# A retention layer in front of a Mish MLP: the first tile's q and k loads split over token groups, and the first tile made of four batches

## The chip, the cores and the metric

The kernel runs on one core of a Trainium2 chip. The metric is the device time in microseconds (us) of one execution; lower is better. The core has TensorE (PE, whose weight loads are listed apart as PEld), VectorE (DVE), ScalarE (ACT), GpSimd (POOL) and SyncE (SP). SP, ACT and POOL can issue DMAs; "SPq", "ACTq" and "POOLq" in the profile are those issuing queues.

## The reference

For each of 8 batches and 8 heads there are 576 tokens with 64 numbers each in q, k and v (float32). The attention has no softmax: it is a retention with a decay per head.

```python
scores = q @ k^T / sqrt(64)                       # 8 batches, 8 heads, 576 x 576
gamma  = 1 - 2 ** (-5 - h)                        # one per head h
ret    = scores * where(i >= j, gamma ** (i - j), 0)
x      = (ret @ v), heads joined to 512 numbers   # 4608 tokens x 512
h      = x @ w_in                                 # 512 -> 2048
out    = (h * tanh(softplus(h))) @ w_out          # 2048 -> 512, float32
```

## The kernel before

**Chunks and tiles.** The 576 tokens of a batch are cut into four chunks of 128 and a rest of 64. A list `chunks` orders all 36 chunks (two rests make one chunk). Two neighbouring chunks are a pair `m`: the same tokens of two batches. Four chunks are a tile `t` of 512 tokens, on which the MLP works; there are nine tiles. In the list before, the chunks 0 to 7 are the tokens 0, 128, 256 and 384 of the batches 0 and 1. So the first tile (chunks 0 to 3) holds tokens 0 to 255 of two batches.

**What is done to a chunk.** The decay is split into a factor for q and one for v, so a chunk needs only a triangular mask. The steps have one letter each:

- P (`step_p`): DVE multiplies q by its factor and casts it to bf16, into `qks`.
- V (`step_v`): v times its factor into `vs`. For the first tile it is POOL that does it, and it first casts k into `qks`.
- T (`step_t`): q and k are transposed, on PE into PSUM and then copied by ACT into `qkT`.
- S (`step_s`): 8 score matmuls into a PSUM tile `sc`, then DVE multiplies by the mask into `sm`.
- O (`step_o`): 8 matmuls `vs` x `sm`, for a chunk that isn't the first of its batch 8 more with the state of the earlier chunks (`ssb`), then a copy into the tile's `xT`.
- N (`step_n`): only for the pairs 0 and 1: k is transposed back into `ks` (8 PE transposes and a copy of 128x1024).
- K (`step_k`): a pair's k and v are added to its batches' state (16 PE matmuls into the PSUM tile `st`, two ACT copies into `ssb`). N must come before it for the pairs 0 and 1.

**The MLP.** `g1` is 4 matmuls against `w_in` and a Mish on ACT into `gT`; `g1_some` and `g1_chunk` do the same for 3 chunks or one. `g2` is `gT` against `w_out`, then a DVE copy and a store.

**Order.** The kernel runs under a manual schedule: each engine does its instructions in the order in which the program writes them, and each queue issues its DMAs in that order. First come the loads of the first tile, then constants, then a loop over the four first chunks (the head), and then everything else (the body): a pass of `g1` over the first tile into which N and K of pair 1 and the chunk 4 are woven, `g1_chunk` passes for the chunks 4 to 7, and alternating `g1` and `g2` with the later chunks.

**Loads.** The first tile is loaded by SP (`load_first`, L128 to L137), all 20 DMAs ahead of everything else. Its q and k are laid out so that one partition holds four consecutive tokens of one head (1 KB): partitions 0 to 31 are head 0 (or 1), 32 to 63 head 2 (or 3), and so on. This is one DMA for the even and one for the odd heads:

```python
in_=heads[b, e, :, ds(i0, P), :].rearrange("p (g t) d -> p g (t d)", t=4)
```

The outer loop of the source is over four heads `p`, the next over 32 token groups `g`. v is loaded with one token in a partition. All other loads are issued by POOL, in the order w_in (0,2), w_in (2,2), then w_in (4,4), w_in (8,4), chunk 4's q, k and v, w_in (12,2), w_in (14,2), chunks 5 to 7, w_out, and the pairs 4, 5, ... The POOL engine also does V of the first tile, so these loads stand behind it in POOL's order: w_in (0,2) behind V of chunk 2, w_in (2,2) and all later ones behind V of chunk 3.

**Filling PE.** `keep_warm(n)` issues n matmuls of 128x512 on zeros: 9 ahead of the head, then 2 before and 3 after each S.

Of the kernel before, what the change touches and what calls it, by code (L numbers as in the profile page):

```python
# [17 lines left out]
def kernel(  # L18
# [31 lines left out]

    chunks = []
    for g in range(0, B, 4):
        for b in (g, g + 2):
            for c in range(4):
                chunks += [((b + u, P * c, P),) for u in range(2)]
        chunks += [((g + u, 512, 64), (g + 2 + u, 512, 64)) for u in range(2)]
    n_chunks = len(chunks)
    n_pairs = n_chunks // 2
# [2 lines left out]
    def place(n):  # L61
        return chunks[n][0][1] // P
# [65 lines left out]
    def load_first(n):  # L128

        b, i0, _ = chunks[n][0]  # L130
        m, u = divmod(n, 2)
        for x, src in (("q", q), ("k", k)):
            heads = src.rearrange("b (p e) s d -> b e p s d", e=2)
            for e in range(2):
                nc.sync.dma_start(out=pairs[m][x][:, u, ds(4 * e, 4), :].rearrange("p t d -> p (t d)"),  # L135
                                  in_=heads[b, e, :, ds(i0, P), :].rearrange("p (g t) d -> p g (t d)", t=4))
        nc.sync.dma_start(out=pairs[m]["v"][:, u], in_=v[b, :, ds(i0, P), :].rearrange("h p d -> p h d"))  # L137

    for n in range(NCH):
        load_first(n)  # L140

# [4 lines left out]
    def keep_warm(n):  # L148
        for _ in range(n):
            nc.tensor.matmul(warm, lhsT=idle[:, 0:P], rhs=idle, start=True, stop=True)  # L150

    keep_warm(9)


    pos1 = consts.tile([P, 2, 4], F32)
    nc.gpsimd.iota(pos1, pattern=[[P, 2], [1, 4]], base=0, channel_multiplier=4,
                   allow_small_or_imprecise_dtypes=True)
    ident = consts.tile([P, P], BF16)
    make_identity(nc, ident)

    pos = consts.tile([P, 5], F32)
    nc.gpsimd.iota(pos, pattern=[[P, 5]], base=0, channel_multiplier=1,
                   allow_small_or_imprecise_dtypes=True)
    nc.gpsimd.iota(pos[64:P, 4:5], pattern=[[1, 1]], base=512, channel_multiplier=1,
                   allow_small_or_imprecise_dtypes=True)
    ex = consts.tile([P, 5, H], F32)
    for h in range(H):
        nc.vector.tensor_scalar(ex[:, :, h], pos, math.log(1.0 - 2.0 ** (-5.0 - h)), None, op0=OP.mult)

    lg1 = consts.tile([P, 2], F32)  # L170
    off1 = consts.tile([P, 1], F32)
    for a in range(NP):
        rows = ds(32 * a, 32)
        nc.vector.memset(off1[rows], 128.0 * a)
        for e in range(2):
            nc.vector.memset(lg1[rows, e:e + 1], math.log(1.0 - 2.0 ** (-5.0 - 2 * a - e)))
    ex1 = consts.tile([P, 2, 2, 4], F32)
    for e in range(2):
        nc.vector.tensor_scalar(ex1[:, :, e, :], pos1, off1, lg1[:, e:e + 1], op0=OP.subtract, op1=OP.mult)
    gq1 = consts.tile([P, 2, 2, 4], F32)  # L180
    nc.scalar.activation(gq1, ex1, AX.Exp)
    gq = consts.tile([P, 5, H], F32)
    gv = consts.tile([P, 5, H], F32)
    nc.scalar.activation(gq, ex, AX.Exp)
    nc.scalar.activation(gv, ex, AX.Exp, scale=-1.0)
    first = consts.tile([P, 1], F32)
    nc.scalar.activation(first, pos[:, 0:1], AX.Mish)
    nc.vector.tensor_scalar(gq, gq, 1.0 / math.sqrt(D), None, op0=OP.mult)
    nc.vector.tensor_scalar(gq1, gq1, 1.0 / math.sqrt(D), None, op0=OP.mult)

    mask = consts.tile([P, P], F32)
    mask2 = consts.tile([P, P], F32)
# [25 lines left out]
    def step_p(m, u0=0, nu=2):  # L218

        r = pairs[m]  # L220
        u = ds(u0, nu)
        if m < NCH // 2:
            nc.vector.tensor_tensor(by_lines(r["qks"][:, 0, u0]), by_heads(r["q"][:, u0]),
                                    gq1[:, place(2 * m)].unsqueeze(3).to_broadcast([P, 2, 4, D]), op=OP.mult)
            return
        g = gq[:, place(2 * m), :].unsqueeze(1).unsqueeze(3).to_broadcast([P, nu, H, D])
        nc.vector.tensor_tensor(r["qks"][:, 0, u], r["q"][:, u], g, op=OP.mult)  # L227

    def step_v(m, u0=0, nu=2):

        r = pairs[m]
        u = ds(u0, nu)
        if "vs" not in r:
            r["vs"] = tok.tile([P, 2, H, D], BF16, name="vs")
        g = gv[:, place(2 * m), :].unsqueeze(1).unsqueeze(3).to_broadcast([P, nu, H, D])
        eng = nc.vector
        if m < NCH // 2:
            eng = nc.gpsimd
            eng.tensor_copy(by_lines(r["qks"][:, 1, u0]), by_heads(r["k"][:, u0]))  # L239
        eng.tensor_tensor(r["vs"][:, u], r["v"][:, u], g, op=OP.mult)  # L240

    def step_t(n):

        m, u = divmod(n, 2)
        r = pairs[m]
        if "qk" not in r:
            r["qk"] = tr.tile([P, 2, 2, NP, P], BF16, name="qkT", bufs=3)
        if n >= NPE:
            nc.scalar.dma_start_transpose(out=r["qk"].rearrange("p i u n t -> p (i u n) t"),  # L249
                                          in_=r["qks"].rearrange("p i u h d -> p (i u h d)"))  # L250
            return
        if n < NCH:
            tp = ps_h.tile([P, 2, NP, P], BF16, name="hp")
            for i in range(2):
                lines = r["qks"][:, i, u].rearrange("p h d -> p (h d)")
                for t in range(4):
                    nc.tensor.transpose(tp[:, i, :, ts(t, 32)], lines[:, ts(t, P)], ident)  # L257

                nc.scalar.copy(r["qk"][:, i, u].rearrange("p n (g t) -> p n g t", t=4),
                               tp[:, i].rearrange("p n (t g) -> p n g t", t=4))  # L260
            return
        tp = ps_sc.tile([P, 4, NP, P], BF16, name="sc")[:, 0:2]
        for i in range(2):
            flat = r["qks"][:, i, u].rearrange("p h d -> p (h d)")
            for p in range(NP):
                nc.tensor.transpose(tp[:, i, p, :], flat[:, ts(p, P)], ident)  # L266
        nc.scalar.copy(r["qk"][:, :, u], tp)  # L267

    def step_n(m):

        r = pairs[m]
        kp = ps_h.tile([P, 2, NP, P], BF16, name="hp")
        for u in range(2):
            for p in range(NP):
                nc.tensor.transpose(kp[:, u, p, :], r["qk"][:, 1, u, p, :], ident)
        r["ks"] = tok.tile([P, 2, H, D], BF16, name="ks", bufs=2)
        nc.scalar.copy(r["ks"].rearrange("p u h d -> p u (h d)"), kp.rearrange("p u n t -> p u (n t)"))

    def step_s(n):

# [35 lines left out]
    def step_o(n):  # L316

        t, s = divmod(n, NCH)
        m, u = divmod(n, 2)
        qk, vs = pairs[m]["qk"], pairs[m]["vs"]  # L320
        sc, sm = pairs[m][u]
        ot = sc[:, 0]
        start = True
        off = 0
        for b, i0, ni in chunks[n]:
            if i0 > 0:
                for p in range(NP):
                    for e in range(2):
                        nc.tensor.matmul(ot[ds(64 * e, 64), p, ds(off, ni)], lhsT=st_sb[b, i0][:, p, e, :],  # L329
                                         rhs=qk[:, 0, u, p, ds(off, ni)],  # L330
                                         start=(start and p == 0), stop=False, skip_group_check=True)
                start = False
            off += ni
        for p in range(NP):
            for e in range(2):
                nc.tensor.matmul(ot[ds(64 * e, 64), p, :], lhsT=vs[:, u, 2 * p + e, :], rhs=sm[:, e, p, :],  # L336
                                 start=(start and p == 0), stop=True, skip_group_check=True)
        if s == 0:
            xts[t] = xp.tile([P, KC, NCH * P], BF16, name="xT")
        nc.vector.tensor_copy(xts[t][:, :, ts(s, P)], ot)  # L340


    gts = {}
# [73 lines left out]
    def one(n, steps):  # L417
        m, u = divmod(n, 2)
        for step in steps:
            if step in "PV":  # L420
                {"P": step_p, "V": step_v}[step](m, u, 1)
            else:
                {"T": step_t, "S": step_s, "O": step_o}[step](n)

    one(0, "PVT")
    for n in range(NCH):
        last = n == NCH - 1
        keep_warm(2)
        if not last:
            one(n + 1, "P")  # L430
        one(n, "S")
        if n == 1:
            step_n(0)
        keep_warm(3)
        if not last:
            one(n + 1, "VT")
            if n > 0:
                load_w_in(2 * n - 2, 2)
            one(n, "O")
            if n == 1:  # L440
                step_k(0)
    load_w_in(4, 4)
    load_w_in(8, 4)
    load_single(4)
# [14 lines left out]
    g1_chunk(3, 0)  # L459
    for i in range(4, nF):  # L460
        if i == 6:
            step_n(1)
        elif i == 8:
            step_k(1)
        elif i == 12:
            one(4, "PVT")
        elif i == 14:
# [24 lines left out]
    def visit(m, w):  # L492

        n = 2 * m
        if w == 0:
            step_p(m)
            step_v(m)
            if 2 * m + 2 < NPE:
                load(m + 4)
        elif w == 2:  # L500
            one(n, "T")
        elif w == 3:
            one(n + 1, "T")
# [88 lines left out]
```

## Time and profile before

| | |
|---|---|
| median of 14 runs (lowest to highest) | 337.33 us (335.22 to 338.87) |
| the profiled execution, its own time | 336.15 us |
| its span | 334.4 us |
| PE busy | 308.7 us (92%) |
| DVE, ACT, POOL busy | 130.8, 126.1, 79.9 us |
| DMA | 43.38 MB moved, 130 GB/s over the span |
| first `g1` matmul on a full tile (L351) | starts at 42.80 us |

The profile is of one execution. Its span runs from the first to the last event on the core; the execution's own time is 1.75 us longer, and the median of the runs is 1.18 us above that. "Busy" counts an engine's instructions; the rows of the timeline and the stage table give times from the span's start. In the stage table "DMA share" is the mean busy share of 16 DMA engines (transfers that overlap in one engine can take it above 1), and the last column is what they moved.

### The profile page before, as it was taken

What the parts mean: (1) busy time and instruction counts of PE and PEld (TensorE: products, weight loads), DVE (VectorE), ACT (ScalarE), POOL (GpSimd) and SP (SyncE); (2) the same over time, 40 slices, a digit from 0 to 9 for tenths busy, and PEclk for the clock granted to TensorE, in tenths of its full rate; (3) what the DMA queues carried; (4) which work ended last, traced back from release to release, by engine and by line L of the source; (5) the groups of instructions that cost most, each with busy time, mean ns of one, the idle gap of its engine ahead of it and who ended that gap; (6) DMA issues with size and microseconds to landing.
All of it is one profiled execution on the core that took longest, in us unless ns stands there. A gap on an engine that the chain in (4) does not pass through costs nothing.

```text
span 334.4 us, 6026 instructions
## 1 busy us (share of the span) xinstructions
PE 308.7 (92%) x2599; PEld 160.5 (48%) x2637; DVE 130.8 (39%) x176; ACT 126.1 (38%) x206; POOL 79.9 (24%) x101
## 2 busy tenths in 40 slices
PE   5466689999999999999999999999999999999996
PEld 1142345896455555444454545444554544444444
DVE  3233214620667467535445262626272723000121
ACT  4132366662234564233442434243433432333300
POOL 2232867635442102140404304050000000000000
PEclk9977999999999999999999999999999999999999
DMA  2335899999999904969598797999241411000023
GB/s 82 109 115 104 123 230 201 207 224 198 246 205 242 210 32 96 194 83 203 143 199 128 173 171 148 139 165 154 61 90 37 110 39 42 33 31 33 31 63 94
DMA packets 75594, 43.38 MB, mean 130 GB/s; under 512 B 59568, under 2 KB 66992, under 8 KB 75568
## 3 DMA queue, kind: packets, MB, share of 16 engines
q0 software_dynamic: 43104, 25.17, 50.8%
q1 hardware_dynamic: 11520, 12.45, 12.2%
q10 hardware_dynamic: 20944, 5.38, 9.9%
q8 instruction: 20, 0.33, 0.4%
q14 instruction: 6, 0.05, 0.0%
HBM read 36.70 MB, written 9.44 MB: 138 GB/s over the span
## 4 chain that ended last, share of the span: by engine, by line
PE 78%; SPq 7%; DMA 5%; ACT 3%; ACTq 3%; DVE 2%; issue 1%; POOL 1%
PE hp L351 30%; PE ops L389 29%; SPq L135 6%; PE hp L389 5%; PE hp L374 4%; PE sc L287 3%; DMA vraw<-in_v_dram 3%; ACTq L249 3%; DMA w_in_t<-in_moe_w_in_dram 3%; PE sc L329 2%; PE sc L336 2%; PE sc L266 2%; PE st L308 1%; ACT gT L353 1%; PE hp L401 1%
## 5 line engine op out<-in xcount | busy, mean ns | idle before, releaser
L351 PE MATMUL hp<-xT,w_in_t 128*128 128x512 bf16 x468 | 123.0, 380 | 5.2 <-DMA w_in_t<-in_moe_w_in_dram 3.1
L353 ACT ACTIVATE gT<-hp 128x512 bf16<-128x512 f32 x124 | 73.9, 598 | 133.5 <-PE hp L351 107.5
L389 PE MATMUL ops<-w_out_t,gT 128*128 128x512 bf16 x476 | 121.3, 379 | 0.7
L389 PEld LDWEIGHTS <-gT 128*128 128x128 bf16 x560 | 54.2, 98 | 64.7 <-issue 0.8
L351 PEld LDWEIGHTS <-w_in_t 128*128 128x128 bf16 x496 | 46.0, 98 | 58.3 <-DMA w_in_t<-in_moe_w_in_dram 3.3
L409 DVE COPY res<-ops 128x512 f32<-128x512 f32 x30 | 20.7, 691 | 129.7 <-PE ops L389 129.7
L290 DVE TENSOR_TENSOR sm<-sc,mask 128x1024 bf16<-128x1024 f32 x36 | 42.6, 1216 | 19.2 <-PE sc L287 19.2
L515 POOL COPY seen<-qkT 1x1 bf16<-1x1 bf16 x10 | 1.8, 177 | 127.0 <-DMA qkT<-qks 127.0
L340 DVE CAST xT<-sc 128x512 bf16<-128x512 f32 x36 | 23.5, 686 | 16.6 <-PE sc L336 15.8
L312 ACT ACTIVATE ssb<-st,diag 128x512 bf16<-128x512 f32 x32 | 20.2, 684 | 10.2 <-PE st L308 10.0
L227 DVE TENSOR_TENSOR qks<-qraw,gq 128x1024 bf16<-128x1024 f32 (+1 forms) x18 | 19.7, 1096 | 9.2 <-DMA qraw<-in_q_dram 9.2
L104 POOL DMA_DIRECT2D qraw<-in_q_dram x16 | 17.2, 1076 | 19.8 <-DVE qks L227 12.8
L240 DVE TENSOR_TENSOR vs<-vraw,gv 128x1024 bf16<-128x1024 f32 (+1 forms) x18 | 19.8, 1099 | 0.9 <-DMA vraw<-in_v_dram 0.9
L104 POOL DMA_DIRECT2D vraw<-in_v_dram x16 | 17.3, 1088 | 6.0 <-DMA w_out_t<-in_moe_w_out_dram 2.5
L389 PE MATMUL hp<-w_out_t,gT 128*128 128x512 bf16 x76 | 18.0, 379 | 0.5 <-issue 0.5
L104 POOL DMA_DIRECT2D qks<-in_k_dram x16 | 17.2, 1082 | 5.1 <-PE hp L374 3.2
L267 ACT COPY qkT<-sc 128x1024 bf16<-128x1024 bf16 x12 | 12.2, 1013 | 14.6 <-PE sc L266 14.6
L374 PE MATMUL hp<-xT,w_in_t 128*128 128x128 bf16 x272 | 16.7, 219 | 0.0
L374 PEld LDWEIGHTS <-w_in_t 128*128 128x128 bf16 x272 | 15.4, 98 | 0.7 <-issue 0.2
L257 PE MATMUL hp<-ident,qks 128*128 128x128 bf16 x32 | 3.6, 242 | 12.1 <-POOL qks L239 9.3
L150 PE MATMUL ops<-idle 128*128 128x512 bf16 x27 | 12.8, 613 | 1.8 <-DVE idle L145 1.3
L336 PE MATMUL sc<-sm,vs 128*64 128x128 bf16 x288 | 14.1, 224 | 0.0
(63 smaller groups left out, 155.6 us busy)
## 6 DMA issues: line engine op xcount, KB each, us to landing
out_dram<-res SPq DMA_DIRECT2D x31, 256.0 KB
qraw<-in_q_dram POOLq DMA_DIRECT2D x12, 512.0 KB, 7.2
vraw<-in_v_dram POOLq DMA_DIRECT2D x12, 512.0 KB, 9.0
qks<-in_k_dram POOLq DMA_DIRECT2D x12, 256.0 KB, 7.7
qraw<-in_q_dram POOLq DMA_DIRECT2D x8, 256.0 KB, 9.8
vraw<-in_v_dram POOLq DMA_DIRECT2D x8, 256.0 KB, 8.3
w_out_t<-in_moe_w_out_dram POOLq DMA_DIRECT2D x4, 512.0 KB, 11.8
qraw<-in_q_dram SPq DMA_DIRECT2D x8, 128.0 KB
```

The lines of the kernel that those rows point to most:

```text
L104: nc.gpsimd.dma_start(out=t[ds(off, ni)].rearrange("p u h d -> p (u h) d"), in_=src[ds(b, 2), :, ds(i0, ni), :].rearrange("b h p d -> p (b ...
L135: nc.sync.dma_start(out=pairs[m][x][:, u, ds(4 * e, 4), :].rearrange("p t d -> p (t d)"), in_=heads[b, e, :, ds(i0, P), :].rearrange("p (g ...
L240: eng.tensor_tensor(r["vs"][:, u], r["v"][:, u], g, op=OP.mult)
L290: nc.vector.tensor_tensor(sm.rearrange("p e n i -> p (e n) i"), sc.rearrange("p e n i -> p (e n) i"), (mask if len(chunks[n]) == 1 else ma ...
L312: nc.scalar.activation(ssb[:, :, :, e, :], st, AX.Copy, scale=diag[:, e:e + 1])
L336: nc.tensor.matmul(ot[ds(64 * e, 64), p, :], lhsT=vs[:, u, 2 * p + e, :], rhs=sm[:, e, p, :], start=(start and p == 0), stop=True, skip_gr ...
L340: nc.vector.tensor_copy(xts[t][:, :, ts(s, P)], ot)
L351: nc.tensor.matmul(hp, lhsT=w_in_t[:, c, ts(f, P)], rhs=xts[t][:, c, :], start=(c == 0), stop=(c == KC - 1))
L353: nc.scalar.activation(gts[t][:, f, :], hp, AX.Mish)
L374: nc.tensor.matmul(hp[:, j, :], lhsT=w_in_t[:, c, ts(4 * fb + j, P)], rhs=xts[t][:, c, ts(s, P)], start=(c == 0), stop=(c == KC - 1))
L389: nc.tensor.matmul(ops, lhsT=gts[t][:, f, ts(s, P)], rhs=w_out_t[:, f, :], start=(f == 0), stop=(f == nF - 1))
L409: copy(ot, ops)
```

## The change

1. **Layout of the first tile's q and k.** The source's outer loop becomes the 32 token groups, the inner one the four heads. The partition of a row is then 4 x group + head pair, where it was 32 x head pair + group. The factors for q (`gq1`) are built for that layout: from the partition number's last two bits and eight compares and a sum on DVE, in place of memsets. The PSUM tile of T is written in whole 128-column blocks, and ACT's copy reads it in another order.
2. **Queue of the first tile's v.** ACT issues it, not SP. Chunk 0 is loaded at the start, chunk 1 behind ACT's exponentials, and chunks 2 and 3 in the head's loop, behind T of the chunks 0 and 1. SP's DMAs wait for nothing.
3. **Order of chunks.** The pair (batches 2 and 3, tokens 0 to 127) becomes pair 1; the pairs after it move back by one, up to the former pair 4. The first tile is then the first 128 tokens of four batches, and none of its chunks needs a state.
4. **N and K leave the head.** N of pair 0, K of pair 0 and N of pair 1 stand in the `g1` pass at i = 6, 8 and 9; K of pair 1 stands in `visit(5, 2)`, some 60 us later. N's copy moves from ACT to DVE and its PSUM tile from the pool of `hp` to that of `sc`. `vs` of the first tile has two buffers of its own.
5. **Small moves.** V is split into C (the cast of k) and V. w_in (2,2) is issued between C and V of chunk 3. The copy of O in the first tile goes from DVE to ACT. `keep_warm` goes to 12 ahead of the head and 4 and 3 around each S. The constants are built in another order.

```diff
-        for b in (g, g + 2):
-            for c in range(4):
-                chunks += [((b + u, P * c, P),) for u in range(2)]
+        order = [(b, c) for b in (g, g + 2) for c in range(4)]
+        if g == 0:
+            order.insert(1, order.pop(4))
+        for b, c in order:
+            chunks += [((b + u, P * c, P),) for u in range(2)]
...
-                                  in_=heads[b, e, :, ds(i0, P), :].rearrange("p (g t) d -> p g (t d)", t=4))
-        nc.sync.dma_start(out=pairs[m]["v"][:, u], in_=v[b, :, ds(i0, P), :].rearrange("h p d -> p h d"))
-    for n in range(NCH):
-        load_first(n)
+                                  in_=heads[b, e, :, ds(i0, P), :].rearrange("p (g t) d -> g p (t d)", t=4))
+        nc.scalar.dma_start(out=pairs[m]["v"][:, u], in_=v[b, :, ds(i0, P), :].rearrange("h p d -> p h d"))
+    load_first(0)
...
-    keep_warm(9)
+    keep_warm(12)
...
+    nc.vector.tensor_scalar(line, line, 3, None, op0=OP.bitwise_and)
+    nc.vector.tensor_copy(off1, line)
+    for a in range(NP):
+        for e in range(2):
+            nc.vector.tensor_scalar(own[:, e, a:a + 1], off1, float(a),
+                                    math.log(1.0 - 2.0 ** (-5.0 - 2 * a - e)), op0=OP.is_equal, op1=OP.mult)
+    nc.vector.tensor_reduce(out=lg1, in_=own, op=OP.add, axis=mybir.AxisListType.X)
...
+    load_first(1)
...
-                    nc.tensor.transpose(tp[:, i, :, ts(t, 32)], lines[:, ts(t, P)], ident)
+                    nc.tensor.transpose(tp[:, i, t, :], lines[:, ts(t, P)], ident)
-                               tp[:, i].rearrange("p n (t g) -> p n g t", t=4))
+                               tp[:, i].rearrange("p t (g n) -> p n g t", n=NP))
...
-        kp = ps_h.tile([P, 2, NP, P], BF16, name="hp")
+        kp = ps_sc.tile([P, 4, NP, P], BF16, name="sc")[:, 0:2]
-        nc.scalar.copy(r["ks"].rearrange("p u h d -> p u (h d)"), kp.rearrange("p u n t -> p u (n t)"))
+        nc.vector.tensor_copy(r["ks"].rearrange("p u h d -> p u (h d)"), kp.rearrange("p u n t -> p u (n t)"))
...
-        nc.vector.tensor_copy(xts[t][:, :, ts(s, P)], ot)
+        (nc.scalar.copy if t == 0 else nc.vector.tensor_copy)(xts[t][:, :, ts(s, P)], ot)
...
-    one(0, "PVT")
+    one(0, "PCVT")
     for n in range(NCH):
         last = n == NCH - 1
-        keep_warm(2)
+        if n + 2 < NCH:
+            load_first(n + 2)
+        keep_warm(4)
         if not last:
             one(n + 1, "P")
         one(n, "S")
-        if n == 1:
-            step_n(0)
         keep_warm(3)
         if not last:
-            one(n + 1, "VT")
-            if n > 0:
-                load_w_in(2 * n - 2, 2)
+            one(n + 1, "C")
+            if n == 2:
+                load_w_in(2, 2)
+            one(n + 1, "V")
+            if n == 1:
+                load_w_in(0, 2)
+            one(n + 1, "T")
             one(n, "O")
-            if n == 1:
-                step_k(0)
...
         if i == 6:
+            step_n(0)
+        elif i == 8:
+            step_k(0)
+        elif i == 9:
             step_n(1)
-        elif i == 8:
-            step_k(1)
...
         elif w == 2:
+            if m == 5:
+                step_k(1)
             one(n, "T")
```

More of the change, by code (lines that the diff above doesn't have):

```diff
@@ L150, in keep_warm @@
             nc.tensor.matmul(warm, lhsT=idle[:, 0:P], rhs=idle, start=True, stop=True)
-    keep_warm(9)
-    pos1 = consts.tile([P, 2, 4], F32)
-    nc.gpsimd.iota(pos1, pattern=[[P, 2], [1, 4]], base=0, channel_multiplier=4,
+    keep_warm(12)
+    line = consts.tile([P, 1], mybir.dt.int32)
+    nc.gpsimd.iota(line, pattern=[[0, 1]], base=0, channel_multiplier=1)
+    pos1 = consts.tile([P, 4], F32)
+    nc.gpsimd.iota(pos1, pattern=[[1, 4]], base=0, channel_multiplier=1,
                    allow_small_or_imprecise_dtypes=True)
-    ident = consts.tile([P, P], BF16)
-    make_identity(nc, ident)
     pos = consts.tile([P, 5], F32)
@@ L165 @@
                    allow_small_or_imprecise_dtypes=True)
+    ident = consts.tile([P, P], BF16)
+    make_identity(nc, ident)
+    nc.vector.tensor_scalar(line, line, 3, None, op0=OP.bitwise_and)
+    off1 = consts.tile([P, 1], F32)
+    nc.vector.tensor_copy(off1, line)
+    own = consts.tile([P, 2, NP], F32)
+    for a in range(NP):
+        for e in range(2):
+            nc.vector.tensor_scalar(own[:, e, a:a + 1], off1, float(a),
+                                    math.log(1.0 - 2.0 ** (-5.0 - 2 * a - e)), op0=OP.is_equal, op1=OP.mult)
+    lg1 = consts.tile([P, 2], F32)
+    nc.vector.tensor_reduce(out=lg1, in_=own, op=OP.add, axis=mybir.AxisListType.X)
+    ex1 = consts.tile([P, 2, 4], F32)
+    for e in range(2):
+        nc.vector.tensor_scalar(ex1[:, e, :], pos1, off1, lg1[:, e:e + 1], op0=OP.subtract, op1=OP.mult)
+    gq1 = consts.tile([P, 2, 4], F32)
+    nc.scalar.activation(gq1, ex1, AX.Exp)
+    nc.vector.tensor_scalar(gq1, gq1, 1.0 / math.sqrt(D), None, op0=OP.mult)
     ex = consts.tile([P, 5, H], F32)
@@ L168 @@
         nc.vector.tensor_scalar(ex[:, :, h], pos, math.log(1.0 - 2.0 ** (-5.0 - h)), None, op0=OP.mult)
[L170 to L181, printed above, removed]
     gq = consts.tile([P, 5, H], F32)
     gv = consts.tile([P, 5, H], F32)
+    nc.scalar.activation(gv, ex, AX.Exp, scale=-1.0)
     nc.scalar.activation(gq, ex, AX.Exp)
-    nc.scalar.activation(gv, ex, AX.Exp, scale=-1.0)
+    nc.vector.tensor_scalar(gq, gq, 1.0 / math.sqrt(D), None, op0=OP.mult)
+    load_first(1)
     first = consts.tile([P, 1], F32)
     nc.scalar.activation(first, pos[:, 0:1], AX.Mish)
-    nc.vector.tensor_scalar(gq, gq, 1.0 / math.sqrt(D), None, op0=OP.mult)
-    nc.vector.tensor_scalar(gq1, gq1, 1.0 / math.sqrt(D), None, op0=OP.mult)
     mask = consts.tile([P, P], F32)
@@ L223, in step_p @@
             nc.vector.tensor_tensor(by_lines(r["qks"][:, 0, u0]), by_heads(r["q"][:, u0]),
-                                    gq1[:, place(2 * m)].unsqueeze(3).to_broadcast([P, 2, 4, D]), op=OP.mult)
+                                    gq1.unsqueeze(3).to_broadcast([P, 2, 4, D]), op=OP.mult)
             return
@@ L227, in step_p, with step_c @@
         nc.vector.tensor_tensor(r["qks"][:, 0, u], r["q"][:, u], g, op=OP.mult)
+    def step_c(n):
+        m, u = divmod(n, 2)
+        r = pairs[m]
+        nc.gpsimd.tensor_copy(by_lines(r["qks"][:, 1, u]), by_heads(r["k"][:, u]))
     def step_v(m, u0=0, nu=2):
@@ L232, in step_v @@
         u = ds(u0, nu)
+        early = m < NCH // 2
         if "vs" not in r:
-            r["vs"] = tok.tile([P, 2, H, D], BF16, name="vs")
+            r["vs"] = (tok.tile([P, 2, H, D], BF16, name="vs1", bufs=NCH // 2) if early
+                       else tok.tile([P, 2, H, D], BF16, name="vs"))
         g = gv[:, place(2 * m), :].unsqueeze(1).unsqueeze(3).to_broadcast([P, nu, H, D])
[L236 to L240, printed above, removed]
+        (nc.gpsimd if early else nc.vector).tensor_tensor(r["vs"][:, u], r["v"][:, u], g, op=OP.mult)
     def step_t(n):
@@ L422, in one @@
             else:
-                {"T": step_t, "S": step_s, "O": step_o}[step](n)
-    one(0, "PVT")
+                {"C": step_c, "T": step_t, "S": step_s, "O": step_o}[step](n)
+    one(0, "PCVT")
     for n in range(NCH):
         last = n == NCH - 1
-        keep_warm(2)
+        if n + 2 < NCH:
+            load_first(n + 2)
+        keep_warm(4)
         if not last:
```

## The prediction

> **What bounds the kernel now.** The page's row of slices says where to look: PE has 9 in nearly every slice from the sixth on, and 4 to 7 in the first five (8.4 us each). So the first 43 us are the only place with much to win. The stage table, cut along that stretch, says what is busy there (columns: stage, length, busy time of PE, PEld, DVE, ACT and POOL, clock, DMA share, GB/s):
>
> ```profile
> 0.00:7.00 7.00, 4.02 (x9) 1.20 (x9) 2.52 (x29) 3.24 (x6) 1.97 (x13) 1.00 0.30 81
> 7.00:14.00 7.00, 4.00 (x21) 1.52 (x21) 0.75 (x2) 1.17 (x2) 1.65 (x2) 1.00 0.40 115
> 14.00:21.00 7.00, 4.18 (x36) 2.31 (x37) 2.80 (x5) 1.85 (x3) 1.65 (x2) 0.76 0.40 115
> 21.00:28.00 7.00, 4.67 (x50) 2.29 (x49) 2.74 (x4) 2.77 (x5) 2.53 (x3) 0.76 0.58 136
> ...
> 35.00:43.00 8.00, 4.33 (x48) 2.72 (x47) 0.69 (x1) 2.56 (x5) 5.84 (x8) 1.00 1.10 162
> 43.00:58.00 15.00, 13.89 (x117) 6.98 (x118) 4.41 (x6) 10.68 (x17) 10.41 (x13) 1.00 1.44 215
> ```
>
> No engine is full in the head, yet DMA moves 115 GB/s there against 215 in the body. PE's 4 us include the zero matmuls. Cutting the third row into single microseconds shows two kinds of load: 1 us in which only q and k are on their way, and 1 us with v:
>
> ```profile
> 16.00:17.00 1.00, 0.00 (x1) 0.01 (x1) 0.00 (x0) 0.00 (x0) 0.61 (x1) 1.00 0.30 86
> ...
> 18.00:19.00 1.00, 1.00 (x8) 0.30 (x8) 0.54 (x1) 0.02 (x1) 0.26 (x1) 0.50 1.07 265
> ```
>
> 86 GB/s at a share of 0.30 is 4 to 5 busy engines of 16, and they are all that carries q and k: four, at 21 GB/s each. Who waits for that is in the list of waits up to 45 us (total, times, longest):
>
> ```profile
> POOL qks L239 <- DMA kraw<-in_k_dram: 20.4, 4, 6.5
> ...
> DVE qks L223 <- DMA qraw<-in_q_dram: 11.8, 4, 6.3
> ```
>
> The chain, from the first DMA of chunk 3's q (start, length, what):
>
> ```profile
> 17.25 2.94 SPq L135
> ...
> 20.23 1.25 SPq L135
> 21.53 1.41 SPq L135
> ...
> 23.56 8.88 DMA vraw<-in_v_dram
> ...
> 32.52 1.04 POOL vs L240
> ...
> 34.30 8.45 DMA w_in_t<-in_moe_w_in_dram
> ```
>
> P starts when q has landed, at 6.63, 13.57, 20.29 and 27.07: 6.8 us for each chunk. SP is held up too: its q DMAs, 0.56 us when free, take up to 2.99. Behind the last chunk stand v (landed at 32.5), POOL's V, and only then w_in (4,4), which lands at 42.75 and starts the body.
>
> **What the Trainium skill says.** "DMA: Bandwidth & Descriptors", section "Why a DMA increments its semaphore by 16 and not by 1": the number of engines is the largest k up to 16 that divides the slowest dimension of both patterns. The source's is 4 heads before, so k = 4, which agrees with the share of 0.27 to 0.30. After, it is 32 groups against 128 partitions: k = 16, which no row of q or k before shows; v (128 on both sides) reached 265 GB/s. The same page, "Issuing engines are not separate DMA queues": v on ACT's queue uses the same 16 engines, so it saves issue time only. "TensorE: Matmul & The Clock Gate", Part 1: PE runs at half rate until it has been busy for a window of about 3.4 us. The trace agrees: the records alternate 0.50 and 1.00 in windows of 3.4 us in the head and stay at 1.00 in the body; zero matmuls step 0.43 us at first, 128x512 matmuls 0.215 warm (0.86 for 4 in the chain).
>
> **Part 1, loads.** q or k of a chunk is 2 DMAs of 128 KB. At 16 engines of 21 GB/s a DMA takes 0.4 us (1.5 before), so SP's issue sets the pace: 0.53 to 0.69 us each, 2.4 us for a chunk's four. The landing of q in chunk 0 before: first bytes about 1.5 us after the issue at 0.81, 256 KB at 85 GB/s, so 5.4, and P starts at 6.63: 1.2 us go by at the end. After: issue ends at 2.2, 1.1 more to the first bytes, 0.4, and 1.2: 4.9. k lands at about 6.1, and q and k of chunk 3 at about 12.1 and 13.3 (27.0 and 30.0 before). v is 256 KB, 1.1 us at 235 GB/s, beside the rest. All 3 MB at 250 GB/s are 12.6 us, so this is consistent.
>
> **The head then becomes a chain of engines.** Start: DVE's constants are two small operations, 8 compares, a sum and 2 more at about 0.1 to 0.24 us (rows L168 and L179), then the exponential at 3.0, 8 multiplications (0.77), gq and three memsets; it is free for P(0) at 5.3. So P(0) waits for DVE, not for q. PE's 12 zero matmuls end at 1.26 + 12 x 0.43 = 6.4. T(0) follows, ACT's two copies (0.58 each) end at 8.2, S(0) starts at 8.4. Then for each chunk, warm: PE 4 + 3 zero matmuls 1.5, S 0.40, T 0.80, O 0.48: 3.2 us; ACT 2 x 0.58, a copy of about 0.65 for O, 0.5 for the issue of v: 2.3; DVE 0.69 + 1.22 = 1.9; POOL 0.61 + 1.04, plus 0.9 where it issues w_in: 2.6. The loop of T, copies, S, mask and O is covered by the zero matmuls. So PE is the pace: S(1) at 11.6, S(2) at 14.7, S(3) at 17.9, first `g1_some` at 18.9 (34.64 before).
>
> **POOL and ACT in the head.** ACT's order puts v of chunk 2 behind T(0)'s copies (8.2) and v of chunk 3 behind O(0)'s copy (11.8): with 0.5 to issue and 3 us to land (1.1, 1.1 and 1.2 as above, a little overlapped) near 11.9 and 15.5. POOL: V(2) ends at 13.0, w_in (0,2), C(3), w_in (2,2) at 14.5, V(3) from 15.5 to 16.6, then w_in (4,4) (34.3 before). What waits behind V(3) on POOL is every later load. With the measured 8.45 us w_in (4,4) lands at 25.0; PE would be ready for it at 23.5 (18.9 + 4 `g1_some` 2.9 + O(3) 0.45 + `g1_chunk` 1.05 + gaps). So the body starts at 25.0 and not 42.8: **minus 17.8 us**. The queue behind w_in (4,4) moves by the same 17.7 us, so the body meets its later loads with the slack that it had (chunk 4's v landed at 48.2, T(4) came at 51.15; w_out landed near 67, `g2` began at 77.4).
>
> **Part 2, what moves from the head into the body.** PE: N(0) 0.61, K(0) 0.44, and state matmuls: pair 4 after (tokens 384) has 2 x 0.41, where the former pair 4 was a batch's first. Sum **plus 1.9 us**, all on PE, which is the bound there. N(1) and K(1) were in the body already. N's copy costs nothing on DVE (128x512 takes 0.69, so 1.2 to 1.4 for 128x1024): DVE is idle between 38 and 46 us of before; it delays P(4) to about 2.5 us behind N(1), with three `g1` (2.6 us) and the transposes ahead of T(4). It takes 1.0 off ACT, where `g1` waited a little. K(1) in `visit(5, 2)` puts 1.26 us of ACT ahead of T(10)'s copies (2 x 1.01), with three `g2` (2.6 us) before S(10): 0 to 0.9 us late, I take 0.4. The order of chunks changes no other count.
>
> **Unknown costs.** ACT's copy with its new read order may be as before (0.58) or slower; a doubling would make ACT's round 3.4 us, 0.2 above PE's: 0 to +1. Eleven further zero matmuls (40 against 29) cost 0.2 to 0.43 each on PE, are in the 3.2 us, and become pure cost only if cold. If q and k slow v or w_in down: 0 to +2.
>
> **Sum.** 334.4 - 17.8 + 1.9 + 0.4 = 318.9 span. With 1.75 around it 320.7, and 1.2 more for the median's distance to the profiled execution: 321.9, or **322 us**.
>
> **Rivals.**
>
> - *Cold head.* PE isn't busy enough in some window, and the head runs at half rate: T, S and O 0.61 for 0.40, zero matmuls 0.43. A round is 5.2 us, 2 us more, for two or three of four rounds: +4 to +6, or 326 to 328. For it: the clock fell three times before. Against: PE waited up to 3 us there for DMA, and these waits go.
> - *Weights late.* V(3) waits for v behind ACT, or w_in (0,2) shares engines with the last q and k (it took 5.5 us from issue before), and all of POOL's queue is later: +2 to +4, 324 to 326.
> - *Faster.* w_in (4,4) finds the engines empty and lands in 6.5 us; then PE is the bound at 23.5, and N's relief of ACT counts: -1 to -3, 319 to 321.
> - *No spread, and slower.* The q and k DMAs stay on four engines. Then chunk 3's k lands at 30 as before and the body starts no more than 1.8 us earlier (V(3) at 31.5 for 32.5, w_in (2,2) ahead of it), while the body's 1.9 to 2.6 us stay: 337.4 to 339.9, at the likeliest 339. It decides if the four chunks together take over 24.6 us to load (27.2 before, less the 2.6): below 128 GB/s in the head. For it: nothing in this trace shows q or k on more engines. Against: v's DMAs, from the same queue, do it.
>
> **How the numbers follow.** A measurement of this kernel can tell about 0.3%, 1 us, from no change. Main case 0.55 (320 to 324), faster 0.15, cold or late 0.23 (324 to 328), no spread 0.05, anything else that eats the gain 0.02. The range 317.5 to 328 leaves out the last two and the ends. Faster 0.93, same 0.02, slower 0.05.
>
> **What would show it.** Right: the DMA share of the first 12 us near 1 and over 200 GB/s; P starts at about 5.3 and then each 3 us; SP's DMAs all issued by 11; first `g1` on a full tile at 25.0; the chain before it through w_in (4,4). The stages from there to the end 2.3 us longer. Wrong: 85 GB/s on q and k; records of 0.50 after 10 us; the chain through ACT's issue of v; PE waiting for q, k or w_out in the body, which would mean that the loads did not move with it.

## The result and the profile after

The changed kernel takes 324.89 us (median of 10 runs, 323.91 to 326.95) against 337.63 us (median of 47 runs). The ratio is 0.9636, with a 95% interval of 0.9612 to 0.966: 3.6% faster. The forecast was 322 us, from 317.5 to 328. The time lies inside the range, but 0.9 us above the main case (320 to 324), in the band of the rivals "cold head" and "weights late" (324 to 328).

The profiled execution, the one at 326.95 us, is the slowest of the ten. Its span is 325.2 us, 6.3 us longer than the forecast span of 318.9. Where these are shows in the start times of the first instruction of each step (us from the span's start; "v early" is the first experiment below):

| step | before | forecast | after | v early |
|---|---|---|---|---|
| P of chunk 0 | 6.63 | 5.3 | 4.76 | 6.06 |
| ACT's first copy of T(0) | 8.02 | about 7 | 10.77 | 7.25 |
| S(0) | 11.62 | 8.4 | 13.62 | 9.06 |
| S(3) | 32.88 | 17.9 | 27.50 | 20.09 |
| first `g1_some` | 34.64 | 18.9 | 28.49 | 21.08 |
| issue of w_in (4,4) | 34.3 | 16.6 | 25.5 | 17.9 |
| first full `g1` (body) | 42.80 | 25.0 | 32.53 | 25.97 |
| span | 334.4 | 318.9 | 325.2 | 318.6 |

The stage table of the changed kernel, cut at its own steps (same columns as before: PE, PEld, DVE, ACT, POOL, clock, DMA share, GB/s):

```profile
0.00:7.50 7.50, 5.73 (x16) 2.28 (x17) 3.92 (x29) 1.85 (x4) 3.70 (x16) 1.00 0.61 173
7.50:11.40 3.90, 0.01 (x1) 0.01 (x1) 0.49 (x1) 1.96 (x3) 0.61 (x1) 0.90 0.78 213
11.40:20.00 8.60, 7.59 (x46) 3.54 (x46) 2.64 (x2) 2.33 (x4) 4.83 (x6) 0.50 0.60 124
20.00:28.50 8.50, 6.99 (x71) 3.52 (x67) 3.60 (x4) 3.32 (x6) 3.97 (x5) 0.95 0.51 75
28.50:32.50 4.00, 4.00 (x41) 2.59 (x40) 0.67 (x1) 2.44 (x5) 4.00 (x6) 1.00 1.24 204
```

The loads are what was forecast: 213 GB/s where only 115 were. The trace's records of DMA completions show the spread itself: each of the 16 q and k DMAs of the first tile landed with four such records before (the first one between 4.44 and 4.75 us) and lands with 16 after (3.67 to 4.27 us). But in the second row little use is made of them: PE is idle for almost 4 us, and DVE and POOL do little more. In the third row PE is busy again, at a clock of 0.50 for the whole stage. (The clock column reads 1.00 ahead of the first record of the clock, which comes at 7.19 us here. It doesn't show that the 12 zero matmuls step at 0.43 us before that, the half rate.) The waits up to 35 us have turned over:

```profile
POOL vs L252 <- DMA vraw<-in_v_dram: 10.7, 3, 5.9
...
PE hp L269 <- ACT qkT L271: 6.4, 4, 4.4
...
ACT L197 <- DMA qraw<-in_q_dram: 5.1, 1, 5.1
...
POOL qks L241 <- DMA kraw<-in_k_dram: 3.6, 2, 2.6
...
DVE qks L231 <- DMA qraw<-in_q_dram: 1.5, 1, 1.5
```

The waits for q and k fell from 11.8 and 20.4 us to 1.5 and 3.6. New is a wait of ACT, an engine that needs no q: L197 is the load of the Mish table, and ahead of it in ACT's order stands the issue of chunk 1's v. The chain says the same (start, length, what):

```profile
6.06 2.89 DMA qraw<-in_q_dram
8.97 0.37 ACTq L140
9.37 1.28 ACT L197
10.87 0.48 ACT qkT L271
11.39 0.58 PE hp L269 x4
...
28.66 1.30 PE hp L374 x8
...
32.96 1.46 PE hp L363 x6
```

Chunk 2's first q lands at 8.95; at 8.97 ACT issues the v of chunk 1, then loads the table, and only then copies q of T(0), whose transposes had been ready since 7. This standstill of ACT is called the hold below. From 11.39 on the chain to the body is PE's and ACT's own; it doesn't pass through w_in (4,4) any more.

Why a v waits for a q is in the trace's records of the instructions, which name the completion counter (semaphore) that each DMA counts up and those that it waits for. The program as built has eight counters for the DMAs of SP and ACT together (100, 102, 103 and 105 to 109) and hands them out in turn; a DMA waits until the one that had its counter before has landed. All of SP's q and k got their turns ahead of ACT's second v:

```
SP   first q DMA of chunk 2    uses counter 102          issued 6.06, landed 8.95
ACT  v of chunk 1              waits for 102, uses it    issued 8.97
DVE  P of chunk 2              waits for 103 and 102     (q of chunk 2)
POOL V of chunk 1              waits for 102             (v of chunk 1)
```

SP's DMAs have the same kind of wait from the eighth on (in the kernel before from the ninth on), but each of these was met before SP came to it, before and after. What makes single issues on SP take up to 2.99 us before (0.69 at most after) is thus something else, which no run here takes apart. On ACT the table load and all copies of T stand behind the wait.

### The profile page after: what moved, and what is told of

Its sections match the earlier page's. It is cut to its first block, busy times and chain, and to the rows that moved or that the text cites. A ratio compares the mean times of both kernels' runs of the same rounds, so it can differ in the third digit from the quotient of the medians.

```text
span 325.2 us, 6053 instructions
## 1 busy us (share of the span) xinstructions
PE 308.7 (95%) x2610; PEld 161.7 (50%) x2648; DVE 131.1 (40%) x173; ACT 126.6 (39%) x208; POOL 79.9 (25%) x102
## 3 DMA queue, kind: packets, MB, share of 16 engines
q1 hardware_dynamic: 7552, 11.41, 11.2%
## 4 chain that ended last, share of the span: by engine, by line
PE 90%; ACT 3%; ACTq 2%; SPq 2%; issue 1%; DVE 1%; DMA 1%
PE hp L363 32%; PE ops L401 31%; PE hp L401 5%; PE hp L386 4%; PE sc L299 3%; PE ops L152 3%; PE sc L348 3%; PE sc L341 2%; PE st L320 2%; ACTq L261 2%; PE sc L278 2%; SPq L138 2%; PE hp L413 1%; ACT qkT L279 1%; DMA qraw<-in_q_dram 1%
## 5 line engine op out<-in xcount | busy, mean ns | idle before, releaser
L352 DVE CAST xT<-sc 128x512 bf16<-128x512 f32 x32 | 20.8, 685 | 6.7 <-PE sc L348 5.9
L252 DVE TENSOR_TENSOR vs<-vraw,gv 128x1024 bf16<-128x1024 f32 (+1 forms) x18 | 19.8, 1098 | 0.0
L152 PE MATMUL ops<-idle 128*128 128x512 bf16 x38 | 14.8, 536 | 1.8 <-DVE line L171 1.3
L299 PEld LDWEIGHTS <-qkT 64*128 64x128 bf16 x288 | 8.3, 96 | 10.5 <-issue 6.8
```

What stands on the lines that cost most here:

```text
L252: (nc.gpsimd if early else nc.vector).tensor_tensor(r["vs"][:, u], r["v"][:, u], g, op=OP.mult)
L352: (nc.scalar.copy if t == 0 else nc.vector.tensor_copy)(xts[t][:, :, ts(s, P)], ot)
```

## The experiments

All times are medians; each ratio is to runs of the kernel before on the same chip, with its 95% interval.

| run | us | ratio (interval) | body from |
|---|---|---|---|
| changed kernel | 324.89 | 0.9636 (0.9612 to 0.966) | 32.53 |
| v early | 320.22 | 0.9508 (0.9477 to 0.954) | 25.97 |
| T split | 322.21 | 0.9557 (0.9526 to 0.9587) | 28.11 |
| 31 zero matmuls | 322.34 | 0.9569 (0.954 to 0.9598) | 28.54 |
| layout back | 334.12 | 0.9926 (0.9895 to 0.9957) | 41.74 |
| layout back, v early | 331.32 | 0.9839 (0.9804 to 0.9874) | 38.98 |
| before + layout alone | 320.21 | 0.952 (0.948 to 0.956) | 28.30 |
| both: v early, T split | 321.04 | 0.9517 (0.9476 to 0.9557) | 24.19 |
| both, w_in first | 318.18 | 0.9446 (0.9413 to 0.9478) | 24.32 |
| both, w_in one chunk earlier | 317.70 | 0.9433 (0.9406 to 0.9461) | 23.67 |
| before + layout + w_in first | 319.74 | 0.9497 (0.9466 to 0.9527) | 27.75 |

The last column is from the one profiled execution of each. Runs in different rows were not all made on one chip; a difference between two rows is given by medians, and by the ratios where the two disagree.

### v of chunk 1 issued early

```diff
-    load_first(1)              # behind ACT's exponentials: q, k and v
+    load_first(0); load_v(1)   # v of chunk 1 right behind v of chunk 0
...
+    load_first(1)              # q and k only
```

> The changed kernel with one move: ACT issues chunk 1's v right behind chunk 0's, ahead of the exponentials, so that no earlier DMA of its completion counter is under way. Theory A (ACT was held: in the changed kernel v of chunk 1 was issued at 8.97 us only, because it waited for chunk 2's q on the same counter, and the table load and T(0)'s copies stood behind it until 10.77): T(0)'s first copy at about 7.0, S(0) near 8.5 to 9 instead of 13.6, the clock doesn't fall back for 10 us, first full g1 at 25 to 27 instead of 32.5, time 318 to 320 us. Rival B (the head's pace is PE's own: cold rounds of 6 us whatever ACT does): S(0) moves, but rounds stay at 5 to 6 us; 322 to 324. Rival C (the loads are the pace: v ahead of q and k costs what it saves): within 1 us of the changed kernel, 324 to 326.

Measured: 320.22 us, T(0)'s first copy at 7.25, S(0) at 9.06, the body from 25.97, and a mean clock of 1.000 in three of four executions. Theory A holds; it missed the time by 0.2 us. Rival B fails (rounds of 3.68 us, not 5 to 6), and so does C: q of chunk 0 is 1.3 us later (P at 6.06 for 4.76), which costs little. The whole distance from the changed kernel, 4.7 us (4.3 by the ratios), comes from one DMA issue at a different place in ACT's order. (The move also lands that v 7 us earlier for POOL, at 5.61 for 12.83, but the chain of the changed kernel didn't pass through it.) The chain is now the one that the forecast had:

```profile
6.07 2.95 DMA qraw<-in_q_dram
9.02 0.02 issue
9.04 4.52 DMA vraw<-in_v_dram
...
13.63 0.75 POOL vs L259
...
16.90 0.99 POOL vs L259
17.89 8.04 DMA w_in_t<-in_moe_w_in_dram
...
25.97 0.39 PE hp L370
```

The first three rows show the same trap once more: v of chunk 2 waits for counter 103 and is issued at 9.04, because the q that had this counter landed at 9.02. ACT had been free for only 0.15 us, so here it costs nothing.

### PE kept busy over the hold

```diff
-    keep_warm(12)
+    keep_warm(31)
```

> The changed kernel with 31 in place of 12 zero matmuls ahead of the head, which keep PE busy over the time in which T(0) stands still; ACT's late start stays. Theory A (of some 7.5 us that the head is longer than forecast, 3 to 4 are the half-rate clock after PE's idle time from 7.0 to 11.4, the rest is ACT): no record of 0.50 after 8 us, S(0) at 13.5 to 14.5 as it was, rounds of 3.7 instead of 6.0 and 4.2, first full g1 at 29 to 30.5, 321.5 to 323 us. Rival (the clock falls back in any case, or PE's rate isn't on the path): rounds as in the changed kernel, 324 to 326 us.

Measured: 322.34 us. ACT waits as before (4.9 us in the list of waits), S(0) starts at 12.49, and the rounds (from one S to the next) are 3.7, 3.7 and 3.7 us. The clock column shows why (stages of this run; from 5.9 us on the zero matmuls step at 0.22 us, the full rate):

```profile
0.00:11.50 11.50, 9.56 (x39) 4.07 (x40) 4.83 (x29) 3.83 (x7) 4.27 (x17) 1.00 0.67 185
11.50:20.00 8.50, 6.83 (x74) 3.62 (x75) 3.84 (x4) 3.90 (x7) 6.30 (x8) 1.00 0.78 157
```

Theory A holds in time and rounds; S(0) and the body come a little earlier than it said, for what stands ahead of S(0) runs at full rate too. So of the 4.7 us that "v early" wins, 2.5 are the clock that fell back (of 4.3, 2.3 by the ratios), and the rest is ACT's lateness by itself. The forecast of 3 to 4 us for the clock was made against the slowest of the ten executions and is a little high.

The ten executions of the changed kernel agree: their mean clocks are 0.994, 0.989 and 0.983, which is one, two and three windows of 3.4 us at half rate in a span of 323 us, and they took 323.9, 324.0 to 325.1, and 326.2 to 327.0 us. The windows are those of 3.413 us that the Trainium skill's "TensorE: Matmul & The Clock Gate", Part 1, gives: the half-rate record of the profiled execution is 10.24 us long, three times 3.41. The same program lost one, two or three of them; what decides how many was not tried.

### T split over two PSUM tiles

```diff
-            tp = ps_h.tile([P, 2, NP, P], BF16, name="hp")
             for i in range(2):
+                tp = ps_h.tile([P, NP, P], BF16, name="hp")
```

> The changed kernel with q's and k's transposes of the first tile in PSUM tiles of their own, so that PE doesn't wait between them for ACT's copy of q (0.67 us in each round of the changed kernel). ACT's late start is left as it is. Theory A (that wait is on PE's path in every round): three rounds shorter by 0.6 to 0.7, first full g1 1.5 to 2.5 us earlier, 322.5 to 323.5 us. Rival (ACT's two copies and the mask are the path, so the wait only moves to S): less than 0.5 us, 324.4 to 325.2.

Measured: 322.21 us, 2.7 us faster than the changed kernel and a little better than theory A. S(0) starts 2 us earlier as well (11.63 for 13.62), which theory A didn't have. T(0)'s k transposes and the four zero matmuls ahead of S(0) now run before the hold ends (until 7.64), where they came after it at half rate in the changed kernel (11.39 to 13.68); behind the hold only T(0)'s two copies are left (10.52 to 11.57). Then come the rounds, 5.2, 3.3 and 3.0 us for 6.0, 4.2 and 3.7. PE's wait between the two halves of T is real: q and k share a tile, so the k transposes (the second row, from the changed kernel) wait until ACT has read q, 0.67 us in each round:

```profile
21.14 0.39 PE L269 MATMUL hp<-ident,qks 128*128 128x128 bf16 x4
22.20 0.38 PE L269 MATMUL hp<-ident,qks 128*128 128x128 bf16 x4 [0.67 <-ACT qkT L271]
```

The same order of waits is in the program before, but there k landed 2.8 to 2.9 us after q, and the wait was never seen.

### The layout put back, with and without the hold

```diff
-  .rearrange("p (g t) d -> g p (t d)", t=4)
+  .rearrange("p (g t) d -> p g (t d)", t=4)     # and constants, PSUM columns and ACT's copy with it
```

> The changed kernel with the layout of the first tile's q and k put back (outer loop over four heads, constants, PSUM columns and ACT's copy as before); v on ACT, the order of chunks, N and K in the body and all else stay changed. Theory A (the gain is the spread over 16 engines): 85 GB/s on q and k again, k of chunk 3 lands near 30 us, first full g1 at 40 to 43, 335 to 340 us, about as the kernel before. Rival (the gain comes from shorter work in the head: no N, K or state, ACT and POOL freed): first full g1 at 33 to 37, 325 to 330 us.

> The changed kernel with the layout put back (as in the run before) and v of chunk 1 issued right behind v of chunk 0, so that ACT isn't held. It prices the rest of the change without the spread and without the hold. Theory A (four engines set the end of the head): S(0) near 11 to 12 instead of 21.5, but k of chunk 3 still lands near 29 to 30, the body starts at 39.5 to 41.5, 332 to 334.5 us, within 1.5 us of the run with the layout back. Rival (the hold is what made that run slow): 328 to 331 us.

Measured: 334.12 and 331.32 us. The first has its body start in theory A's range (41.74) and is 0.9 us faster than its times. But there is a second reason in it for being slow: with q on four engines again, chunk 2's q lands far later, and the hold lasts until then. Its list of waits:

```profile
ACT L192 <- DMA qraw<-in_q_dram: 13.3, 1, 13.3
PE hp L264 <- ACT qkT L266: 11.9, 3, 10.5
```

With v early the hold is gone and the end of the head is k of chunk 3, as the theory said (chain of that run):

```profile
18.56 10.10 DMA kraw<-in_k_dram
...
28.79 0.61 POOL qks L243
...
29.45 0.61 PE hp L271 x4
```

But 331.32 us lies between theory A's times and the rival's, 2.8 us and not 1.5 from the run before, S(0) comes at 13.26, not at 11 to 12, and the body starts at 38.98, not at 39.5 to 41.5. Everything in the change but the layout is thus worth 5.2 us without the spread (ratio 0.9839), if ACT isn't held, and 2.4 if it is. The hold alone costs 2.8 us here and 4.7 with the spread. Much of the head ran at half rate in both profiled executions (from 7.59 to 28.07 us in the first), so a cost of the clock, which no run takes apart, is in both times.

### The layout alone on the kernel before

> The kernel before with the layout of the first tile's q and k alone changed (token groups as outer loop, its constants, PSUM columns and ACT's copy); all loads on SP, N, K and the order of chunks as before, so the body is that of before. Theory A (the spread is the gain, the rest of the change is not needed for it): SP has issued its 20 DMAs by about 13 us, V(3) ends near 17 to 18, w_in (4,4) lands at 26 to 28, and with the body's 291.6 us of before the time is 319 to 323 us, at least as fast as the whole change. Rival (the head's own work, N, K and the state on PE and ACT, is the next bound): body from 31 us on, 324 to 330 us.

Measured: 320.21 us. Theory A's time holds, in its stronger form: **one part of the change, alone, is 4.7 us faster than the whole** (3.9 by the ratios, whose intervals don't meet). Its chain ends where the forecast for the whole change had it, in v of chunk 3, POOL and w_in (4,4):

```profile
13.12 5.09 DMA vraw<-in_v_dram
...
18.29 1.04 POOL vs L245
19.33 0.75 POOL w_in_t L120
20.08 8.18 DMA w_in_t<-in_moe_w_in_dram
...
28.30 2.53 PE hp L356 x8
```

N, K, the state matmuls and 29 zero matmuls are still in the head here, and S(3) starts at 18.89, a microsecond earlier than with v early and all the rest (20.09). So they are not what ends this head: it ends with w_in (4,4), 3 us after PE's last `g1_chunk` matmul. (The profiled execution is the slowest of the six, at 322.63 us, with a half-rate record from 29.44 to 32.85 in its body.) Together with "v early" at 320.22 this says that once the loads are spread, the rest of the change adds nothing that can be measured, and the hold takes 4.7 us away.

### Both moves, and the weights ahead of v

"Both" is v early with T split. The next two change POOL's order (chunk n + 1 in the loop's pass n):

```diff
             one(n + 1, "C")
+            if n == 1: load_w_in(0, 2)                        # w_in first
+            if n == 2: load_w_in(2, 2); load_w_in(4, 4)
             one(n + 1, "V")
```

The last has (0,2), (2,2) and (4,4) at n = 0, 1 and 2.

> The changed kernel with both moves: v of chunk 1 issued early, and q's and k's transposes in PSUM tiles of their own. Theory A (with v early the chain to the body runs through v of chunks 2 and 3, POOL and w_in (4,4), not through PE): rounds of 3.0 instead of 3.7 us, S(3) at 17.5 to 18, but w_in (4,4) lands at 25.3 to 26 as with v early alone; 319.6 to 320.4 us, within 0.6 of it. Rival (PE is the path): 1.5 to 2.5 us faster than with v early alone, 317.7 to 318.7.

> The run with both moves, and on POOL w_in (0,2) ahead of V of chunk 2, w_in (2,2) and w_in (4,4) ahead of V of chunk 3, so that the weights don't wait for v. Theory A (v and POOL ahead of w_in (4,4) are what is left of the head): w_in (4,4) issued near 15.5 and landed at 23.5 to 24.5, body from 24 on, 317.5 to 319 us. Rival (w_in then takes engines from the last q, k and v, or the engines' rate sets the landing): 319 to 321 us.

> The run with both moves, and each weight load on POOL one chunk earlier: w_in (0,2) ahead of V of chunk 1, w_in (2,2) ahead of V of chunk 2, w_in (4,4) ahead of V of chunk 3. Theory A (the first 2 MB of w_in are limited by the engines' rate once they are issued: 8.3 us from issue to landing with w_in (0,2) and (2,2) just ahead of it): w_in (4,4) finds its forerunners done and lands 1 to 2 us earlier, body from 22.8 to 23.5, 316.5 to 317.5 us. Rival (w_in takes engines from the last chunks' q, k and v, so V, S and the rounds slip by as much): 318 to 320 us.

Measured: 321.04, 318.18 and 317.70 us. "Both" is not settled: its profiled execution, at 318.28 us, is the fastest of six and shows rounds of 3.0 us and a body from 24.19, but four of the six lost a clock window (mean clock 0.994 to 0.995) and took 321.0 to 321.8. Neither theory had that; its interval overlaps that of v early. With w_in first no execution shows a lost window (0.999 and more in all six). Theory A's numbers hold there: w_in (4,4) was issued at 15.97, landed at 24.3, and the time is in its range. Yet the landing is no earlier than in the profiled execution of "both", where it was issued 1.1 us later (8.30 us from issue to landing for 7.04). So issuing it earlier no longer helped, as the rival's second half has it; whether the engines' rate sets the landing is not shown. With each load one chunk earlier, w_in (4,4) is issued even later (16.89), but its forerunners have landed by 18.4, and it lands at 22.3, 2.0 us earlier, as theory A said. The weights are off the path; from 19.8 us on the chain is PE's:

```profile
19.80 1.30 PE hp L381 x8
21.10 0.34 PE sc L355 x8
21.45 1.41 PE hp L381 x8
22.85 0.98 PE hp L393 x16
23.84 0.21 PE hp L370
```

The rival was right in part here as well: chunk 3's k, beside w_in, lands 2 us later (C at 16.34 for 14.38), and S(3) starts at 18.65 for 17.86. With gain and loss together, body (23.67) and time end 0.2 us above theory A's ranges. This was the fastest version, 5.7% below the kernel before; its distance to "w_in first" (0.5 us, with intervals that overlap) is too small to tell.

### The small version

The kernel before with the new layout and "w_in first".

> The kernel before with two edits: the new layout of the first tile's q and k, and on POOL w_in (0,2) ahead of V of chunk 2, w_in (2,2) and w_in (4,4) ahead of V of chunk 3. No other part of the change. Theory A (with the spread, what is left ahead of the body is w_in (4,4) behind V of chunk 3, here 18.3 to 20.1 us): w_in (4,4) issued at 17 instead of 20.1, body from 25 to 26.5 instead of 28.3, 317.5 to 319.5 us. Rival (the order of chunks, N and K in the body and v on ACT are worth something once w_in is early): slower than the run with both moves and w_in first (318.2) by over 1 us, 319.2 to 320.5.

Measured: 319.74 us, body from 27.75. The number is the rival's, but this run doesn't answer the question. In its profiled execution PE's transposes and scores take 0.6 us for 0.4 until 16.5 us, where the first record of the clock comes, so rounds 0 and 1 last 5.2 us; PE became the path, and w_in (4,4), landed at 25.0, was no longer waited for. This start at half rate isn't in the mean clock, which is 1.000 for this execution (320.02 us); the four with 0.989 to 0.995 took less, 319.06 to 319.89. So a mean clock near 1 doesn't say that a head ran at full rate. With nine zero matmuls instead of twelve, and fewer between the steps, PE may be too idle to get its full rate early. That this is the reason was not tried, and "layout alone", with the same zero matmuls, has its first record at 5.54 us.

## Why the prediction was right, and where not

- **What bounds the head: right.** Four engines carried q and k, and the spread is the gain: the layout alone gives a ratio of 0.952, the change without it 0.9839 at best. k = 16, which no row before had shown, is what "DMA: Bandwidth & Descriptors" in the Trainium skill, section "Why a DMA increments its semaphore by 16 and not by 1", derives from the slowest dimensions; here it shows as 16 completions of each DMA for 4, and as 211 and 231 GB/s in the stages from 4 to 8 and 8 to 12 us, for 136 and 114 before. The DMA share there is 0.70 and 0.86, not quite the forecast "near 1". An issue on SP takes 0.58 to 0.69 us, and the last ends at 11.2, about as worked out. ACT's copy with its new read order takes 0.58 us as before, so that unknown cost was none.
- **"8.2: ACT's two copies end": wrong, and the largest miss.** I priced ACT's issue of v at 0.5 us (it takes 0.37 to 0.42) and never asked what that issue would wait for, though it stands ahead of all copies of T. It waits 4.7 us for a DMA of another queue. S(0) came 5.2 us late. The list of what would show the forecast wrong had this line ("the chain through ACT's issue of v"), but the sum had no term for it.
- **"A round is 3.2 us": wrong twice.** At full rate it is 3.68, because T has PE wait 0.67 us for ACT between q and k; I had put T at 0.80, and it takes 1.45. And in the changed kernel it is 6.0, 4.2 and 3.7, because PE's idle 4 us gave away the clock. That rival, "cold head", was priced at 4 to 6 us; the clock alone is 2.5 in the median. Its "against" (PE's waits for DMA go) came true and overlooked a wait of ACT.
- **"The body starts at 25.0": 32.53.** S(0) is 5.2 late, the rounds up to the first `g1_some` 4.4, and 2.0 came back, since w_in (4,4), though issued 9 us later than forecast (v of chunk 3 was issued at 17.92 and took 6.5 us to land beside w_in, for 3), landed at 30.8, before PE was ready. With the hold taken away, the forecast's chain through v, POOL and w_in (4,4) comes true, but late: S(3) and the first `g1_some` by 2.2 us, the issue of w_in (4,4) by 1.3, the body by 1.0. That the span agrees within 0.3 us is luck: from the body to the end it takes 292.6 us for the forecast 293.9, which makes up for it.
- **"The body's later loads move with it": right.** The passes over chunks 4 to 7 last 19.11 us in both kernels, and no PE wait for q, k or w_out appears in the body.
- **"Plus 1.9, plus 0.4": 1.1, too high.** Body to end is 292.7 us, 291.6 before. Busy times of short matmuls overlap with what follows; from start to start N takes 0.45 (I took 0.61), K 0.37 (0.44), eight state matmuls 0.22 (0.41), twice. That is 1.3, not 1.9. By stage: `g1` pass -0.3, though one N more stands in it (a wait of PE for ACT's Mish of 0.24 us is gone, as N's copy left ACT; the rest is not accounted for), `g2` to the third tile's `g1` +0.6, the rest +0.8, where PE waits 1.8 us for a Mish behind ACT's DMA transpose, for 0.8 before. Why that is longer was not tried.
- **"No spread, and slower: 337.4 to 339.9": wrong.** With the layout put back 334.1 us was measured, and 331.3 without the hold. The failing term is the same one: from the body to the end these runs take 292.1 and 292.3 us, 0.5 and 0.7 more than before and not 1.9 to 2.6. That the body starts no more than 1.8 us earlier came true only with the hold (1.1); without it, it is 3.8. Both profiled executions are also slower than their medians, by 1.4 and 1.7 us.

So the spread, the main mechanism, was right, but that the time fell into the range is in part luck: errors of 7.5 us in the head (in the profiled execution) fitted into what the range held for a cold or late head. ACT's late start, which was not among the cases, stood behind most of them, for the clock fell back in the idle time that it made.

## What to carry to other kernels

Before a DMA issue moves to an engine that computes, find out what the issue itself will wait for, its shared completion counter included: a wait that costs nothing on SP can stop everything behind it on an engine that computes. When a load gets much faster, the waits that it had covered come up (here a shared PSUM tile, v behind POOL, weights behind v), so price the next late thing for each engine in order, and try the core of the change alone. An idle time of 4 us on PE cost more than itself here, since the clock fell back for one to three windows of 3.4 us, 2.5 us in the median.

## What was not expected of the hardware

- DVE copied N's 128x1024 bf16 from PSUM in 0.69 us, as long as 128x512 in float32 (0.69); ACT needed 1.01 for the same copy before. The forecast had 1.2 to 1.4.
- DVE's P takes 0.68 to 0.69 us when no V of POOL runs beside it, and 1.00 and 1.50 in the changed kernel where one did (1.47 and 0.91 with v early). In each of these four it ended 0.55 to 0.56 us after V did, though it had begun 0.1 to 0.7 us after V: it hardly got on while V ran. In the kernel before it never met V and took 0.69 each time. It was not on the path.
